# Decode attention over 16 heads: one column of one V block loaded by sixteen row transfers

## The chip, the cores and the metric

The kernel runs on one core of a Trainium2 chip. The metric is the device time of one execution in microseconds (us), the median of several runs. The core has a matrix engine (TensorE, PE in the profile; PEld is its loading of weights), a vector engine (VectorE, DVE), a scalar engine (ScalarE, ACT), GpSimd (POOL) and SyncE (SP). Each takes its own instruction stream in order, and they wait for each other through semaphores. Transfers between HBM (the device memory) and SBUF (the on-chip memory of 128 partitions) are issued by an engine's queue and carried out by 16 DMA engines.

## The reference

One query per head attends over 8192 keys, for 16 heads of width 256, in bf16:

```python
B, H, Sq, Sk, D = 1, 16, 1, 8192, 256
scale = q.shape[-1] ** -0.5
scores = jnp.einsum("bhqd,bhkd->bhqk", q, k) * scale
p = _softmax(scores, axis=-1)
return jnp.einsum("bhqk,bhkd->bhqd", p, v)
```

K and V are 4 MB per head each, 134 MB in all, and every byte is used once.

## The kernel before

**Layout.** For one head, the 8192 rows of K or of V are laid over the 128 partitions, 64 rows to a partition (`J = 64`). A partition so holds 64 "columns" of 256 bf16 values, 512 bytes each, which lie side by side in HBM too: a whole head is 32 KB per partition. There are two buffers for K and two for V (`kbuf`, `vbuf`), and head `h` uses buffer `h % 2`.

**Loads.** SyncE issues all loads of K and V in the order of the list `stream` (lines 57 to 69), in the loop at lines 128 to 138. For heads 2 to 15 it first issues the K of the head two further on, then the V of the head itself. Before the first part of a V it waits until the weighted sum of the head that used the buffer before is done (line 135, semaphore `pv`); so V of head 13 waits for the sum of head 11, V of head 14 for head 12, V of head 15 for head 13. Most V blocks come in one transfer. Head 13 (`V_HALVED`, line 16) comes in two halves of 32 columns, with the semaphores `va1` and `v1h`; head 14 in four pieces of 16 columns; head 15 in seven pieces that begin at columns 0, 16, 32, 44, 52, 58 and 62 (`V_LATE`, line 17). Every transfer covers all 128 partitions and raises its semaphore by 16 when it has landed. Behind the last part of V of head 13, the next thing in SyncE's list is the first piece of head 14, with its wait.

**Scores.** VectorE multiplies 48 of the 64 columns of K by the query and sums each (`head`, line 189). TensorE transposes the other 16 columns, four at a time (`ktrans`), ScalarE copies them out of PSUM (`evac`), and TensorE multiplies them by the query (`kscore`).

**Softmax and weighted sum.** The maximum, the exponentials `E` and their sum are made between the engines in small steps. Then `pv` (line 250) runs 64 matmuls on TensorE, one for each column of V, which add up in PSUM. Ahead of column `j` TensorE waits for what `waits` lists for `j`. ScalarE scales the result and stores it with a transfer of one row of 512 bytes (line 399).

**Order on TensorE.** The loop at line 339 runs nine turns. A turn has the scores of an even head, the weighted sum of the even head two before, the scores of an odd head, and the weighted sum of the odd head two before. The last turn has only the sums of heads 14 and 15. The waits are the same instructions in every turn; which count they wait for is worked out from the turn (`fin_turn`, `half_turn`), and GpSimd raises the semaphores at the start (lines 164 to 167), so that a wait which has no transfer in a turn is met at once. In the sum of an odd head the waits stand ahead of columns 16, 32, 44, 52, 58 and 62 for head 15's pieces, and ahead of column 32 for the second half of head 13.

Of the kernel before, what the change touches and what calls it, by code (L numbers as in the profile page):

```python
# [11 lines left out]
NPE = 16  # L12
# [28 lines left out]
def bass_standalone__mha_softmax__decode_kernel(nc: bass.Bass, q: bass.AP, k: bass.AP, v: bass.AP, out: bass.AP):  # L41
    B, H, Sq, D = q.shape
    Sk = k.shape[2]
    P = 128
    J = Sk // P
# [6 lines left out]
    HALF = J // 2  # L52
# [4 lines left out]
    stream = [("k", 0, 0, K_FIRST, "k0"), ("k", 0, K_FIRST, J, "k0b"), ("k", 1, 0, J, "k1")]  # L57
    stream += [("v", 0, 0, HALF, "va0"), ("k", 2, 0, J, "k0"), ("v", 0, HALF, J, "v0c")]
    stream += [("v", 1, 0, HALF, "va1"), ("k", 3, 0, J, "k1"), ("v", 1, HALF, J, "v1c")]
    for h in range(2, H):  # L60
        if h + 2 < H:
            stream.append(("k", h + 2, 0, J, f"k{h % 2}"))
        if h in V_LATE:
            for (a, b), name in zip(zip(V_LATE[h], V_LATE[h][1:] + (J,)), V_SEMS[h % 2]):
                stream.append(("v", h, a, b, name))
        elif h == V_HALVED:
            stream += [("v", h, 0, HALF, "va1"), ("v", h, HALF, J, "v1h")]
        else:
            stream.append(("v", h, 0, J, f"va{h % 2}"))

    with contextlib.ExitStack() as ctx:
# [9 lines left out]
        def sem(name):  # L81
            if name not in sems:
                sems[name] = ctx.enter_context(nc.semaphore(name))
            return sems[name]
# [29 lines left out]
        for name in ("l", "rc", "pv", "fin", "ldq", "k0", "k0b", "k1", "va0", "va1", "v1h", "o0", "o1"):  # L114
            sem(name)
        late = [name for row in V_SEMS for name in row[1:] if name not in ("v0c", "v1c")] + ["v1h"]
        for row in V_SEMS:
            for name in row[1:]:
                sem(name)

        def src(t, h):
            return t[0, h].rearrange("(p j) d -> p (j d)", p=P)

        if True:

            @(lambda f: f(nc.sync))
            def _(sp):
                for kind, h, a, b, name in stream:
                    buf = (kbuf if kind == "k" else vbuf)[h % 2]
                    if h >= 2 and a == 0:  # L130
                        if kind == "k":
                            sp.wait_ge(sem("kd"), h)
                            sp.wait_ge(sem("tp"), (h - 1) * NG)
                        else:
                            sp.wait_ge(sem("pv"), h + 1)
                    sp.dma_start(  # L136
                        buf[:, a * D : b * D], src(k if kind == "k" else v, h)[:, a * D : b * D]
                    ).then_inc(sem(name), 16)
                sp.nop()

            @(lambda f: f(nc.gpsimd))
            def _(pool):
                def step(ins, n):
                    ins.then_inc(sem("pool"), 1)
                    pool.wait_ge(sem("pool"), n)

                def eye(t, n, done):
                    step(pool.memset(t[:, :], 0.0), n)
                    pool.affine_select(
                        out=t[:, :],  # L150
                        in_=t[:, :],
                        compare_op=ALU.not_equal,
                        fill=1.0,
                        base=0,
                        pattern=[[-1, P]],
                        channel_multiplier=1,
                    ).then_inc(sem(done), 1)

                eye(identb, 1, "cb")
                eye(ident, 2, "cf")  # L160
                pool.memset(ones_row[:, :], 1.0).then_inc(sem("cf"), 1)
                pool.memset(ones_col[:, :], 1.0).then_inc(sem("cf"), 1)
                pool.memset(q_all[:, H * QW : (H + 1) * QW], 0.0).then_inc(sem("cf"), 1)
                for name, n in AHEAD.items():
                    pool.nop().then_inc(sem(name), n)
                for name in late + ["o0", "o1", "va0", "va1"]:
                    pool.nop().then_inc(sem(name), 32 if name in ("o0", "o1") else 16)

# [54 lines left out]
            def _(pe):  # L223
                def transpose_m(h):
                    pe.wait_ge(sem("m"), h.of(1, 2))
                    pe.matmul(  # L226
                        mx[0:1, 0:P], lhsT=m[:, h.par : h.par + 1], rhs=ident[:, :], start=True, stop=True
                    ).then_inc(sem("mT"), 1)

                def bcast(h):  # L230
                    pe.wait_ge(sem("g"), h.of(1, 2))
                    pe.matmul(  # L232
                        sm[:, 0:1],
                        lhsT=ones_row[0:1, 0:P],
                        rhs=g[0:1, h.par : h.par + 1],
                        start=True,
                        stop=True,
                    ).then_inc(sem("bc"), 1)

                def total(h):  # L240
                    pe.wait_ge(sem("ex"), h.of(1, 3))
                    pe.matmul(  # L242
                        qps[0:1, 0:1],
                        lhsT=lsum[:, h.par : h.par + 1],
                        rhs=ones_col[:, 0:1],
                        start=True,
                        stop=True,
                    ).then_inc(sem("l"), 1)

                def pv(h, waits, at):  # L250

                    pe.wait_ge(sem("fin"), h.of(1, 3))
                    pe.wait_ge(sem(f"va{h.par}"), h.of(8, 32 - 8 * h.par))
                    for j in range(J):
                        for name, value in waits.get(j, ()):
                            pe.wait_ge(sem(name), value)
                        ins = pe.matmul(  # L257
                            acc[h.par][0:1, 0:D],
                            lhsT=E[h.par][:, j : j + 1],
                            rhs=vbuf[h.par][:, j * D : (j + 1) * D],  # L260
                            start=(j == 0),
                            stop=(j == J - 1),
                        )
                        if j == J - 1:
                            ins.then_inc(sem("pv"), 1)
                        if j + 1 in at:
                            at[j + 1]()
# [33 lines left out]
                def scores(t, before=None):  # L301
                    if before:
                        transpose_m(before)
                    for gi in range(NG):
                        ktrans(t, gi)
                        if gi >= 1:
                            kscore(t, gi - 1)
                        if gi == 1 and before:
                            bcast(before)
                    kscore(t, NG - 1)  # L310
                    if before:
                        total(before)
# [26 lines left out]
                with pe.Fori(0, H // 2 + 1) as i:  # L339
                    ev, od = _Step(0, i), _Step(1, i)  # L340
                    fin_turn = pe.snap((i // 8) * 16 + 16)
                    half_turn = pe.snap(((i + 1) // 8) * 16 + 16)
                    old = od.back(2)
                    with pe.If(i < H // 2):
                        scores(ev)
                    with pe.If(i > 0):
                        pv(
                            ev.back(2),
                            {V_LATE[14][n]: [(V_SEMS[0][n], fin_turn)] for n in range(1, len(V_SEMS[0]))},
                            {32: lambda: transpose_m(old), 48: lambda: bcast(old), 64: lambda: total(old)},  # L350
                        )
                    with pe.If(i < H // 2):
                        scores(od, before=ev)
                    with pe.If(i > 0):
                        waits = {V_LATE[15][n]: [(V_SEMS[1][n], fin_turn)] for n in range(1, len(V_SEMS[1]))}
                        waits[HALF].append(("v1h", half_turn))
                        pv(old, waits, {})

            @(lambda f: f(nc.scalar))
# [120 lines left out]
```

## Time and profile before

| | us |
|---|---|
| median of 3 runs | 320.71 (320.42 to 320.89) |
| the profiled execution | 321.04 |
| its span, from the first to the last instruction | 319.6 |
| TensorE busy in the span | 220.9 (69%) |
| VectorE busy | 274.9 (86%) |
| ScalarE busy | 92.0 (29%) |

How to read the rows. Line numbers are those of the kernel (L257 is line 257). "out<-in" names what an instruction writes and reads. SPq and ACTq are the queues in which SyncE and ScalarE issue transfers. In the chain of waits and in a timeline the first number is the start in us from the span's start, the second the length, and x32 says that 32 instructions are merged. In a list of issues the last number is the time from the issue to the landing. In a row of stretches stand the stretch, its length, the busy time and the count of PE, PEld, DVE, ACT and POOL, then the granted TensorE clock as a share of full speed, the busy share of the DMA engines, and GB/s. In a row for one source line, three numbers with slashes are the shortest, the median and the longest duration in ns.

### The profile page before, as it was taken

How to read it: one execution, taken by the hardware profiler on the slowest of the kernel's cores; microseconds unless marked ns; L12 is line 12 of the kernel's file. 1: busy time of each engine (PE TensorE's matmuls, PEld its weight loads, DVE VectorE, ACT ScalarE, POOL GpSimd, SP SyncE). 2: the span in 40 equal slices, each digit the busy share in tenths (PEclk: the TensorE clock that was granted, in tenths of full speed). 3: DMA queues.
4: the chain of work that ended last, by engine and by line, in shares of the span. 5: the costliest groups of instructions: out<-in, count | busy, mean ns of one | idle time of the engine just before them, and what ended most of it. 6: DMA issues, size and time to landing. Idle time of an engine off the chain costs nothing.

```text
span 319.6 us, 6845 instructions
## 1 busy us (share of the span) xinstructions
PE 220.9 (69%) x2162; PEld 156.3 (49%) x2162; DVE 274.9 (86%) x1584; ACT 92.0 (29%) x171; POOL 1.6 (0%) x11
## 2 busy tenths in 40 slices
PE   4427186797875947849297573966749477397997
PEld 1326154565554635626256352653626355265675
DVE  2799999999999998897979979889797997979910
ACT  5436050433224060510506123060231605116010
POOL 1000000000000000000000000000000000000000
PEclk9999999769598786969769598785969969587799
DMA  8999999999999999999999999999999999999994
GB/s 329 451 397 455 392 453 416 416 427 435 439 418 443 431 435 439 418 439 427 439 435 423 439 418 443 431 431 435 427 439 414 447 435 427 439 406 423 422 399 179
DMA packets 6549, 134.29 MB, mean 420 GB/s; under 512 B 752, under 2 KB 912, under 8 KB 1424
## 3 DMA queue, kind: packets, MB, share of 16 engines
q1 hardware_dynamic: 6480, 134.22, 98.3%
q8 instruction: 2, 0.03, 0.0%
q10 hardware_dynamic: 64, 0.02, 0.0%
q14 instruction: 3, 0.02, 0.0%
HBM read 134.23 MB, written 0.01 MB: 420 GB/s over the span
## 4 chain that ended last, share of the span: by engine, by line
DMA 49%; PE 24%; DVE 23%; issue 2%; ACT 1%; ACTq 0%; SPq 0%; DVEq 0%
DMA vbuf<-in_v_dram 45%; PE acc L257 23%; DVE kbuf L189 22%; DMA kbuf<-in_k_dram 4%; DVE S L189 1%; PE sm L232 1%; ACT KT L367 1%; PE mx L226 0%; ACT o_sb L392 0%; ACT q_now L362 0%; DVE g L173 0%; SPq L136 0%; PE spe L292 0%; ACTq L399 0%; DVE recip L178 0%
## 5 line engine op out<-in xcount | busy, mean ns | idle before, releaser
L189 DVE CUSTOM_DVE_ANT_0 kbuf<-kbuf,q_now 128x256 bf16<-128x256 bf16 x768 | 268.1, 413 | 22.2 <-DMA kbuf<-in_k_dram 21.2
L257 PE MATMUL acc<-vbuf,E 128*1 128x256 bf16 x1024 | 147.6, 315 | 36.3 <-DMA vbuf<-in_v_dram 36.3
L257 PEld LDWEIGHTS acc<-vbuf,E 128*1 128x1 bf16 x1024 | 96.7, 96 | 80.4 <-DMA vbuf<-in_v_dram 37.3
L367 ACT ACTIVATE KT<-tp 128x1024 bf16<-128x1024 bf16 x64 | 63.8, 1018 | 30.3 <-PE tp L278 30.1
L189 DVE DVE_READ_ACCUMULATOR2_ANT S<- 128x1 f32 x768 | 58.4, 76 | 0.0
L278 PE MATMUL tp<-identb,kbuf 128*128 128x128 bf16 x512 | 42.3, 239 | 13.9 <-DMA kbuf<-in_k_dram 13.8
L292 PE MATMUL spe<-q_now,KT 128*128 128x1 bf16 x512 | 23.1, 166 | 32.3 <-ACT KT L367 31.6
L278 PEld LDWEIGHTS tp<-identb,kbuf 128*128 128x128 bf16 x512 | 33.5, 107 | 18.3 <-DMA kbuf<-in_k_dram 12.4
L292 PEld LDWEIGHTS spe<-q_now,KT 128*128 128x128 bf16 x512 | 18.0, 100 | 42.0 <-ACT KT L367 32.0
L392 ACT ACTIVATE o_sb<-acc,recip 1x256 bf16<-1x256 f32 x16 | 7.4, 464 | 99.9 <-PE acc L257 98.6
L375 ACT ACTIVATE negb<-sm 128x1 f32<-128x1 f32 x16 | 2.8, 172 | 84.5 <-PE sm L232 84.5
L173 DVE TENSOR_REDUCE g<-mx 1x1 f32<-1x128 f32 x16 | 4.4, 276 | 9.8 <-PE mx L226 9.8
L226 PE MATMUL mx<-ident,m 128*1 128x128 f32 x32 | 6.3, 279 | 5.7 <-DVE m L206 5.7
L232 PE MATMUL sm<-g,ones_row 1*128 1x1 f32 x32 | 6.2, 262 | 4.1 <-DVE g L173 4.1
L232 PEld LDWEIGHTS sm<-g,ones_row 1*128 1x128 f32 x32 | 4.9, 190 | 6.2 <-DVE g L173 4.7
L362 ACT ACTIVATE q_now<-q_all 128x258 bf16 (+1 forms) x17 | 7.0, 412 | 0.3 <-DVE S L189 0.3
L178 DVE RECIPROCAL recip<-qps 1x1 f32<-1x1 f32 x16 | 2.4, 151 | 3.9 <-PE qps L242 3.9
L379 ACT ACTIVATE E<-S,negb 128x64 bf16<-128x64 f32 x16 | 5.6, 348 | 0.5
L226 PEld LDWEIGHTS mx<-ident,m 128*1 128x1 f32 x32 | 2.2, 83 | 6.3 <-DVE m L206 5.9
L329 PE MATMUL acc<-q_sb,identb 16*128 16x256 bf16 x16 | 4.4, 403 | 1.0 <-ACT q_all L412 1.0
L371 ACT ACTIVATE S<-spe 128x16 f32<-128x16 f32 x16 | 2.9, 183 | 7.3 <-PE spe L292 7.3
L412 ACT ACTIVATE q_all<-acc 128x512 bf16<-128x512 f32 x8 | 4.4, 593 | 0.9 <-PE acc L329 0.9
(20 smaller groups left out, 16.6 us busy)
## 6 DMA issues: line engine op xcount, KB each, us to landing
kbuf<-in_k_dram SPq DMA_DIRECT2D x15, 4096.0 KB, 20.5
vbuf<-in_v_dram SPq DMA_DIRECT2D x11, 4096.0 KB, 29.0
vbuf<-in_v_dram SPq DMA_DIRECT2D x6, 2048.0 KB, 24.4
vbuf<-in_v_dram SPq DMA_DIRECT2D x6, 1024.0 KB, 12.8
kbuf<-in_k_dram SPq DMA_DIRECT2D x1, 3072.0 KB, 11.7
kbuf<-in_k_dram SPq DMA_DIRECT2D x1, 1024.0 KB, 4.8
vbuf<-in_v_dram SPq DMA_DIRECT2D x1, 768.0 KB, 9.1
vbuf<-in_v_dram SPq DMA_DIRECT2D x1, 512.0 KB, 9.9
```

What stands on the lines that cost most here:

```text
L173: dve.tensor_reduce(g[0:1, h.par : h.par + 1], mx[0:1, 0:P], AX.X, ALU.max).then_inc(sem("g"), 1)
L189: ins = dve.tensor_tensor_reduce(out=buf[:, j * D : (j + 1) * D], in0=buf[:, j * D : (j + 1) * D], in1=q_now[h.par][:, 0:D], scale=SCALE, ...
L226: pe.matmul(mx[0:1, 0:P], lhsT=m[:, h.par : h.par + 1], rhs=ident[:, :], start=True, stop=True).then_inc(sem("mT"), 1)
L232: pe.matmul(sm[:, 0:1], lhsT=ones_row[0:1, 0:P], rhs=g[0:1, h.par : h.par + 1], start=True, stop=True,).then_inc(sem("bc"), 1)
L257: ins = pe.matmul(acc[h.par][0:1, 0:D], lhsT=E[h.par][:, j : j + 1], rhs=vbuf[h.par][:, j * D : (j + 1) * D], start=(j == 0), stop=(j == J ...
L278: ins = pe.transpose(tp[gi % 2][:, b * D + hf * P : b * D + (hf + 1) * P], buf[:, j * D + hf * P : j * D + (hf + 1) * P], identb[:, :],)
L292: ins = pe.matmul(spe[:, c : c + 1], lhsT=KT[gi % 2][:, b * D + hf * P : b * D + (hf + 1) * P], rhs=q_now[h.par][:, D + hf : D + hf + 1], ...
L329: ins = pe.matmul(acc[pair % 2][:, (h % 2) * D : (h % 2 + 1) * D], lhsT=identb[0:H, h : h + 1].to_broadcast([H, P]), rhs=q_sb[:, :], start ...
L362: act.activation(out=q_now[h.par][:, :], in_=src_q, func=ACT.Copy).then_inc(sem("qb"), 1)
L367: act.activation(out=KT[gi % 2][:, :], in_=tp[gi % 2][:, :], func=ACT.Copy).then_inc(sem("kt"), 1)
L379: act.activation(out=E[h.par][:, :], in_=S[h.par][:, :], func=ACT.Exp, bias=negb[:, h.par : h.par + 1], scale=1.0, accum_out=lsum[:, h.par ...
L392: act.activation(out=o_sb[h.par][0:1, :], in_=acc[h.par][0:1, 0:D], func=ACT.Copy, scale=recip[0:1, h.par : h.par + 1],).then_inc(sem("fin ...
```

## The change

The second half of V of head 13 loses its last column, and that column (128 partitions by 512 bytes) comes behind it in sixteen transfers over 1, 2, 3 and so on to 15 partitions and at last over 8, which are 128 together. They share a new semaphore, `dg`, which they raise by 256 in all. TensorE waits for it ahead of the 64th column in the sum of every odd head; GpSimd raises it by 256 at the start for the turns before.

```diff
         elif h == V_HALVED:
-            stream += [("v", h, 0, HALF, "va1"), ("v", h, HALF, J, "v1h")]
+            stream += [("v", h, 0, HALF, "va1"), ("v", h, HALF, J - 1, "v1h")]
+            stream.append(("rows", h, J - 1, J, "dg"))
...
+        sem("dg")
...
+                    if kind == "rows":
+                        r = 0
+                        for n in list(range(1, NPE)) + [8]:
+                            sp.dma_start(
+                                buf[r : r + n, a * D : b * D], src(v, h)[r : r + n, a * D : b * D]
+                            ).then_inc(sem(name), 16)
+                            r += n
+                        continue
...
+                pool.nop().then_inc(sem("dg"), 256)
...
+                    rows_turn = pe.snap(((i + 1) // 8) * 256 + 256)
...
                         waits[HALF].append(("v1h", half_turn))
+                        waits[J - 1] = [("dg", rows_turn)]
```

## The prediction

> **What bounds the kernel now.** I read the page first, then the chain of waits over the last 80 us, then the issues of SyncE's queue one by one with their time to landing, and last the matmuls of the final heads.
>
> ```profile
> span 319.6 us, 6845 instructions
> ...
> DMA  8999999999999999999999999999999999999994
> ...
> DMA packets 6549, 134.29 MB, mean 420 GB/s; under 512 B 752, under 2 KB 912, under 8 KB 1424
> ...
> q1 hardware_dynamic: 6480, 134.22, 98.3%
> ...
> q10 hardware_dynamic: 64, 0.02, 0.0%
> ```
>
> Over the whole span the 16 DMA engines are the bound: SyncE's queue (q1) keeps them 98.3% busy. At 420 GB/s one engine moves 420/16 = 26 GB/s, so 512 B take it 0.02 us. But the change touches only head 13 and what comes behind it, so the question is what bounds the last 45 us:
>
> ```profile
> 247.26 29.66 DMA vbuf<-in_v_dram
> ...
> 276.97 6.03 PE acc L257 x32
> ...
> 293.47 13.27 PE acc L257 x96
> ...
> 310.88 7.02 PE acc L257 x64
> ...
> 317.98 0.47 ACT o_sb L392
> ```
>
> The last transfer on this chain is the V of head 12 (issued at 247.26, landed 29.66 us later). From 276.97 on, the chain is TensorE's work and some copies of ScalarE: the weighted sums of heads 12, 13, 14 and 15 one after another, with the scores of head 15 between. No transfer behind head 12's V stands in it. How near do those transfers come? First the matmuls of heads 13 and 15, and the stretch across the end of head 13:
>
> ```profile
> 293.43 9.82 PE L257 MATMUL acc<-vbuf,E 128*1 128x256 bf16 x64
> ...
> 302.87 3.87 PE L257 MATMUL acc<-vbuf,E 128*1 128x256 bf16 x34
> ...
> 310.74 7.15 PE L257 MATMUL acc<-vbuf,E 128*1 128x256 bf16 x64
> ...
> 293.40:303.00 9.60, 9.60 (x66) 6.38 (x65) 9.60 (x57) 0.17 (x1) 0.00 (x0) 0.71 1.00 416
> ...
> 298.95:303.20 4.25, 4.25 (x41) 3.27 (x40) 4.25 (x25) 0.00 (x0) 0.00 (x0) 1.00 1.00 414
> ```
>
> One matmul lasts 0.27 us and they overlap, so head 15's 64 columns start every (7.15 - 0.27)/63 = 0.109 us: column c at 310.74 + 0.109c. Head 13 is slower, 9.82 us, since the granted clock (the third number from the right) was 0.71 over its stretch and 1.00 only from 298.95 on; its last column starts at 293.43 + 9.82 - 0.27 = 302.98. Now the transfers, issue by issue (start and length of the issue, then size and us to landing):
>
> ```profile
> 266.95 0.43 SPq L136 DMA_DIRECT2D vbuf<-in_v_dram  x1
> vbuf<-in_v_dram SPq DMA_DIRECT2D x1, 2048.0 KB, 29.5
> ...
> 287.14 0.33 SPq L136 DMA_DIRECT2D vbuf<-in_v_dram  x1
> vbuf<-in_v_dram SPq DMA_DIRECT2D x1, 1024.0 KB, 11.8
> ...
> 288.46 0.43 SPq L136 DMA_DIRECT2D vbuf<-in_v_dram  x1
> vbuf<-in_v_dram SPq DMA_DIRECT2D x1, 1024.0 KB, 17.9
> ...
> 303.28 0.33 SPq L136 DMA_DIRECT2D vbuf<-in_v_dram  x1
> ...
> 305.28 0.44 SPq L136 DMA_DIRECT2D vbuf<-in_v_dram  x1
> vbuf<-in_v_dram SPq DMA_DIRECT2D x1, 384.0 KB, 10.2
> ...
> 305.76 0.45 SPq L136 DMA_DIRECT2D vbuf<-in_v_dram  x1
> vbuf<-in_v_dram SPq DMA_DIRECT2D x1, 256.0 KB, 10.3
> ...
> 306.25 0.45 SPq L136 DMA_DIRECT2D vbuf<-in_v_dram  x1
> vbuf<-in_v_dram SPq DMA_DIRECT2D x1, 128.0 KB, 10.1
> ```
>
> The second half of head 13's V lands at 266.95 + 29.5 = 296.45; its 64th column is used at 302.98, **6.5 us later**. Head 14's first piece lands at 298.9 and can't be used before 303.09, 4.2 us later; its last lands at 288.46 + 17.9 = 306.4 and is used at 303.09 + 48 x 0.109 = 308.3 at the earliest, 1.9 us later. In head 15 the 384 KB piece (columns 52 to 57) lands at 315.5 for a start at 316.4, the 256 KB piece at 316.1 for 317.1, the 128 KB piece at 316.35 for 317.5. So the smallest cover in the tail is about **0.95 us**, and a delay of all transfers behind head 13 shows in the end only beyond it.
>
> **The change part by part.**
>
> The half transfer of head 13 loses one column in 32: 128 rows of 512 B, 8 rows an engine, 8 x 0.02 = **-0.16 us** on every engine. Nobody waits for this half at its landing.
>
> Sixteen transfers come onto q1 right behind it: 128 data packets of 512 B, and a completion packet for each engine that takes part. How many take part is seen at two ends only: the 752 packets under 512 B are 45 transfers of SyncE by 16 (720), 16 for the load of q, and one for each of the 16 stores of one row, so 128 rows report from 16 engines and one row from one. Evenly spread, an engine gets 8 rows; in the worst case one engine gets all 128. I take sixteen rows for the busiest, one of each transfer, which is what follows if every transfer begins at the same engine and gives one row to each. [...]
>
> The price of one row with its completion: bytes alone, 0.02 us, are the lower end. The upper end is the 128 KB piece: it lands 316.35 - 316.06 = 0.29 us, say 0.3, behind the 256 KB one, and within that each engine wrote 8 packets of 1 KB and one completion. A pair of one packet and one completion can't be shown from it to cost less than 0.3, though 0.3/8 = 0.04 us is what a packet cost with its share. I take **0.04**: 128 KB at 420 GB/s are 0.31 us, so the completion left no time over. Busiest engine: 16 x 0.04 - 0.16 = **+0.48 us**, between 16 x 0.02 - 0.16 = +0.16 and 16 x 0.3 - 0.16 = +4.6; with 128 rows on one engine at 0.04 it is 5.1 - 0.16 = +5.0. The work that hides +0.48 is TensorE's queue of matmuls in heads 13, 14 and 15, by the 6.5, 1.9 and 0.95 us above; without that cover it is 0.48 us on the end. On the path: **0**.
>
> ```profile
> L136 SPq DMA_DIRECT2D vbuf<-in_v_dram x28: 327/432/643, 2.1 to 306.3; - x28
> ...
> L399 ACTq DMA_DIRECT2D out_dram<-o_sb x16: 230/231/493, 61.0 to 318.5; - x16
> ...
> L256 PEldq FUSED_REGOPS  x24: 83/83/97, 45.5 to 313.2; - x24
> ...
> L167 POOLq EVENT_SEMAPHORE  x12: 17/17/17, 2.8 to 3.7; - x12
> ```
>
> SyncE issues sixteen more transfers. A one-row transfer takes ScalarE's queue 0.23 us, SyncE's own take 0.33 to 0.64: 3.7 to 10.2 us, and 16 x 0.43 = 6.9 by the median. The last one before them ends at 266.95 + 0.43 = 267.38 and the next thing on SyncE is head 14's first piece, which goes at 287.14, when head 12's sum is done. 19.8 us of waiting stand there, so each issue may cost 1.23 us before head 14 is late at all. Path: **0**.
>
> TensorE waits once more in every odd head, ahead of its 64th column, at 0.083 us of its sequencer each. Queued behind it are that head's last matmul, the signal that lets SyncE load head 15, and the next head. In all odd heads but 13 the count was reached before, so only the instruction is left. Two fall into the tail, heads 13 and 15: 0.17 us if nothing covered them. But the stretch from 302.87 crosses the end of head 13, the loop's turn and head 14's first wait and still has (3.87 - 0.27)/33 = 0.109 us a matmul, like head 15 with its six waits: the sequencer runs ahead. Path: 0, at most 0.17; I take **0.05**. GpSimd's extra signal is 0.017 us at 3 us; the first such wait comes at 45.5.
>
> Sum: 0 + 0 + 0.05. On the profiled execution (321.04 us, of which 319.6 are the span) 321.1; this run lies 0.33 over the median of 320.71, so the forecast is **320.8 us, no change that shows**.
>
> [...]
>
> **The rivals.**
>
> *Completions that don't overlap (slower).* On one engine a new completion may follow only when the one before has been taken. For: nothing in the trace puts completions closer than 0.3 us apart on an engine within q1. Against: there eight packets stood between and time was left for none. It decides from (0.95 + 0.16)/16 = 0.07 us a pair, if the busiest engine is also the last; at 0.3 the end moves by 4.6 - 0.95 = 3.7 us, to 324.4.
>
> *A queue that takes only so many transfers (slower).* At 306.25 eight are under way (head 14's last and seven of head 15), and no issue is longer than 0.64. The change has up to 20: head 12's V, head 15's K, two halves and sixteen. With room for eight, only four small ones go in at once, the others as landings make room, the last behind 296.45; then head 14's pieces are issued near 300 instead of from 287.14, the engines stand empty about 5 us, and the end comes 5 - 0.95 = 4 us later, 324.7. Against: nothing shows such a bound.
>
> *Sixteen transfers one behind the other (slower, far).* A transfer alone takes this long:
>
> ```profile
> q_sb<-in_q_dram ACTq DMA_DIRECT2D x1, 8.0 KB, 2.9
> ```
>
> In a row they would end at 296.45 + 16 x 2.9 = 342.9; the 64th column is wanted at 302.98, so 360. The pieces of head 15, landing 0.3 to 0.6 apart after 10 us each, speak against it.
>
> *Faster.* The engines that get fewer than 8 of the 128 rows are done up to 0.16 us sooner. That is under 0.1% even if the end hung on them, and it does not: 0.95 us of TensorE lie over it. A real gain needs the clock: from 293.43 to 298.95 head 13 ran at half speed, where 5.5 us gave the work of 2.8, so a shifted low stretch could give up to 2.7 us, 318.0. Against: the change leaves TensorE's idle times as they are, and the three runs lie within 0.47 us. That the added edits do nothing seen is the forecast itself.
>
> **How the numbers follow.** Forecast 0.73, completions 0.14, bounded queue 0.06, one behind the other 0.02, clock 0.05. About 0.2% (0.64 us) is what a measurement tells from no change. Of the forecast 0.70 stay within it, 0.02 above, 0.01 below; of the clock case 0.04 below, 0.01 within. Slower 0.02 + 0.14 + 0.06 + 0.02 = 0.24, same 0.71, faster 0.05. The forecast's own range is 320.2 to 321.3; to hold 8 in 10 it is stretched over the lower half of the first rival, to 323.0.
>
> **What would show it.** In the new profile: small packets up from 752 by 128 if every row reports from its own engine (q1 6480 + 256); sixteen short issues behind 267.4, done before 279; head 13's last small transfer landing before 302.98; head 14's first issue still at the end of head 12's sum; the chain from 276.97 on TensorE's alone. Wrong if the 64th column waits for a transfer, if head 15's pieces land over 0.95 us later, or if the tail gets or loses a stretch of low clock.

## The result, and the profile after

The changed kernel takes 321.9 us (median of 19 runs, 321.72 to 322.26) against 320.47 us for the kernel before (19 runs on the same chip). The ratio is 1.0038, 95% interval 1.0029 to 1.0047: slower by 0.9 to 1.5 us, which is small but beyond the 0.2% that can be told from no change. The profiled execution agrees: its span is 320.5 us, 0.9 us longer. The lowest of the 19 times is 1.60 us above the lowest before (320.12), the highest only 0.28 us above the highest before (321.98).

The page of the changed kernel counts the packets:

```profile
span 320.5 us, 6870 instructions
...
DMA packets 6805, 134.29 MB, mean 419 GB/s; under 512 B 880, under 2 KB 1168, under 8 KB 1680
...
q1 hardware_dynamic: 6736, 134.22, 98.2%
```

880 packets under 512 B are 752 + 128, and 6736 on SyncE's queue are 6480 + 256: each of the 128 rows brings one data packet and one completion packet. The bytes are the same.

SyncE's timeline from 264 us on, and the chain of waits over the last 72 us, of the changed kernel:

```profile
267.27 5.63 SPq L141 DMA_DIRECT2D vbuf<-in_v_dram  x16
286.99 19.50 SPq L146 DMA_DIRECT2D vbuf<-in_v_dram  x11
```

```profile
248.76 28.18 DMA vbuf<-in_v_dram
...
276.99 5.86 PE acc L268 x32
...
293.32 9.70 PE acc L268 x64
...
303.04 0.33 SPq L146
...
303.41 9.70 DMA vbuf<-in_v_dram
...
313.15 1.91 PE acc L268 x16
315.06 0.13 issue
315.19 3.67 PE acc L268 x32
318.93 0.46 ACT o_sb L405
```

SyncE needs 5.63 us for the sixteen issues (0.35 each) and is done at 272.9; head 14's first piece goes at 286.99, as before (287.14). Up to 293.32 the chain is that of before. Then a transfer stands in it that was not there: one issued at 303.41, the second piece of head 15, which lands at 313.11. In the kernel before, that piece had this row (its issue, and behind it its size and time to landing):

```profile
303.65 0.43 SPq L136 DMA_DIRECT2D vbuf<-in_v_dram  x1
vbuf<-in_v_dram SPq DMA_DIRECT2D x1, 1024.0 KB, 7.7
```

It landed at 311.35. TensorE's timeline of the changed kernel shows what the later landing does:

```profile
310.67 1.91 PE L268 MATMUL acc<-vbuf,E 128*1 128x256 bf16 x16
313.15 5.69 PE L268 MATMUL acc<-vbuf,E 128*1 128x256 bf16 x48 [0.57 <-DMA vbuf<-in_v_dram]
```

Head 15 starts at 310.67 (before 310.74). Column 16 would start at 310.67 + 16 x 0.109 = 312.41 and starts at 313.15, 0.74 us late; the last 48 columns then take 5.69 us where 47 x 0.109 + 0.27 = 5.39 would do, because the later pieces are late too. Head 15's matmuls end at 318.84, and before at 317.89. That is the whole 0.95 us.

Which transfers are late? Issues of the changed kernel one by one, as the prediction showed them for before:

```profile
266.80 0.43 SPq L146 DMA_DIRECT2D vbuf<-in_v_dram  x1
vbuf<-in_v_dram SPq DMA_DIRECT2D x1, 1984.0 KB, 29.7
...
288.33 0.43 SPq L146 DMA_DIRECT2D vbuf<-in_v_dram  x1
vbuf<-in_v_dram SPq DMA_DIRECT2D x1, 1024.0 KB, 19.8
...
306.04 0.44 SPq L146 DMA_DIRECT2D vbuf<-in_v_dram  x1
vbuf<-in_v_dram SPq DMA_DIRECT2D x1, 128.0 KB, 12.1
```

The second half of head 13 lands at 296.5 as before (296.45). Head 14's last piece lands at 308.13 (before 306.36) and head 15's last at 318.14 (before 316.35): **everything behind the sixteen lands about 1.8 us later**, and the amount neither grows nor shrinks from head 14 to head 15. So it is lost at one place. Three stretches, the first of the changed kernel alone, the others of both, changed kernel first:

```profile
290.00:293.50 3.50, 2.33 (x44) 1.75 (x43) 3.50 (x21) 2.92 (x7) 0.00 (x0) 0.75 1.00 427
293.50:296.50 3.00, 3.00 (x16) 1.78 (x15) 3.00 (x19) 0.00 (x0) 0.00 (x0) 0.50 1.03 331
296.50:300.00 3.50, 3.50 (x24) 2.31 (x23) 3.50 (x21) 0.00 (x0) 0.00 (x0) 0.70 0.97 382
```

```profile
293.50:296.50 3.00, 3.00 (x15) 1.78 (x15) 3.00 (x19) 0.07 (x1) 0.00 (x0) 0.50 0.94 396
296.50:300.00 3.50, 3.50 (x23) 2.23 (x21) 3.50 (x21) 0.00 (x0) 0.00 (x0) 0.65 1.01 421
```

The last two numbers are the busy share of the DMA engines and the GB/s. Where the small transfers pass, the engines count as fully busy but move 331 and 382 GB/s instead of 396 and 421. Over these 6.5 us that is (65 x 3.0 + 39 x 3.5) = 332 KB less, 0.8 us at 420 GB/s as a mean over 16 engines; the last engine is 1.8 us late. A busy share of 1.03 at 331 GB/s, against 0.94 at 396 before, says here that an engine holds a packet, not that bytes flow. The trace's records of single packets show which are held. In the changed kernel a packet of 512 B takes 0.027 us and a completion 0.009 (before: 0.009), and such pairs pass as little as 0.03 us apart; but an 8 KB packet of head 14 behind them takes up to 1.63 us, where none took more than 0.32 over the same stretch (293 to 304 us) in the kernel before. Behind 304 us single packets take up to 0.9 us in both kernels.

### The profile page after: what moved, and what is told of

It is laid out like the page before. It is cut to its first block, busy times and chain, and to the rows that moved or that the text cites. A ratio compares the mean times of both kernels' runs of the same rounds, so it can differ in the third digit from the quotient of the medians.

```text
span 320.5 us, 6870 instructions
## 1 busy us (share of the span) xinstructions
PE 220.1 (69%) x2162; PEld 155.5 (49%) x2162; DVE 274.9 (86%) x1584; ACT 91.9 (29%) x171; POOL 1.6 (0%) x11
## 3 DMA queue, kind: packets, MB, share of 16 engines
q1 hardware_dynamic: 6736, 134.22, 98.2%
## 4 chain that ended last, share of the span: by engine, by line
DMA 51%; DVE 23%; PE 22%; issue 2%; ACT 1%; SPq 0%; ACTq 0%; DVEq 0%
DMA vbuf<-in_v_dram 48%; DVE kbuf L200 22%; PE acc L268 20%; DMA kbuf<-in_k_dram 4%; DVE S L200 1%; PE sm L243 1%; ACT KT L380 1%; PE mx L237 0%; SPq L146 0%; ACT o_sb L405 0%; ACT q_now L375 0%; DVE g L184 0%; PE spe L303 0%; ACTq L412 0%; DVE recip L189 0%
## 5 line engine op out<-in xcount | busy, mean ns | idle before, releaser
L289 PE MATMUL tp<-identb,kbuf 128*128 128x128 bf16 x512 | 41.5, 237 | 14.5 <-DMA kbuf<-in_k_dram 14.5
```

Source lines behind the costliest of these rows:

```text
L289: ins = pe.transpose(tp[gi % 2][:, b * D + hf * P : b * D + (hf + 1) * P], buf[:, j * D + hf * P : j * D + (hf + 1) * P], identb[:, :],)
```

## The experiments

What is compared is **the lag**: the landing of head 14's last piece less the landing of head 12's V, both in the same profiled execution, so that a shift ahead of head 12 drops out. It is 306.36 - 276.92 = 29.44 us before and 308.13 - 276.94 = 31.19 after. The lag of an experiment, less 29.44, is what its edit costs the transfers. Times and lags of all runs follow, with the ratio to the kernel before on the same chip. That kernel's own median lay between 320.47 and 321.32 on the chips used, so medians of different rows are not compared:

| run | what column 64 of head 13 does | lag | median | ratio (95%) |
|---|---|---|---|---|
| before | part of the half | 29.44 | 320.47 | |
| changed | 16 transfers, 1 to 15 and 8 rows | 31.19 | 321.90 | 1.0038 (1.0029 to 1.0047) |
| e1_waits | part of the half; only TensorE's wait added | 29.42 | 320.89 | 0.9999 (0.9979 to 1.0020) |
| e2_one | 1 transfer, 128 rows | 29.53 | 320.71 | 0.9997 (0.9979 to 1.0015) |
| e3_even8 | 8 transfers, 16 rows each | 30.31 | 321.50 | 1.0016 (0.9999 to 1.0033) |
| e4_row1 | 16 transfers of 1 row, 1 of 112 | 30.18 | 321.09 | 1.0006 (0.9992 to 1.0021) |
| e5_sems | as e3_even8, a semaphore each | 30.24 | 321.15 | 1.0004 (0.9988 to 1.0020) |
| e6_wide | last 16 columns in 8 transfers of 16 rows | 33.39 | 325.32 | 1.0136 (1.0107 to 1.0165) |
| e7_double | columns 63 and 64, 32 transfers | 33.06 | 324.28 | 1.0109 (1.0083 to 1.0134) |
| e8_early | the 16 transfers in head 5 | 29.44 | 322.19 | 1.0038 (1.0020 to 1.0056) |
| e9_stride | as e5_sems, every eighth row | 30.09 | 321.17 | 1.0019 (1.0009 to 1.0029) |
| e10_wide_stride | as e6_wide, every eighth row | 33.56 | 324.11 | 1.0112 (1.0090 to 1.0134) |
| e11_spread | the 16 transfers in four groups | 30.00 | 321.61 | 1.0037 (1.0018 to 1.0057) |
| e12_eight | last 16 columns in 8 transfers of 8 rows, half of the partitions left out | 29.14 | 320.66 | 0.9981 (0.9961 to 1.0001) |

The theory after the result: the price of a completion on its engine was set too low. Its rivals: TensorE's added wait and register work; the small packets themselves; the number of completions in all; the semaphore that all share, or neighbouring rows; and, where sizes differ, the bytes.

**e1_waits.** The loads go back to two halves, and GpSimd meets the wait of all turns; TensorE's instructions stay.

```diff
-            stream += [("v", h, 0, HALF, "va1"), ("v", h, HALF, J - 1, "v1h")]
-            stream.append(("rows", h, J - 1, J, "dg"))
+            stream += [("v", h, 0, HALF, "va1"), ("v", h, HALF, J, "v1h")]
...
-                pool.nop().then_inc(sem("dg"), 256)
+                pool.nop().then_inc(sem("dg"), 512)
```

> Only TensorE's extra wait ahead of each 64th column and its register work stay; the column comes with the second half again, as before, and no small transfer is issued. Completion theory (each completion that an engine must write for a tiny transfer costs it about 0.19 us): nothing is left that costs, ratio 1.000 within 0.001, and the last piece of V of head 14 lands 29.4 us behind the V of head 12, as before (changed kernel: 31.2). Rival, the wait and register work on TensorE: the whole loss stays, ratio 1.003 to 1.004.

The lag is 29.42 and the ratio 0.9999. The wait costs nothing that shows; the interval leaves room for 0.6 us.

**e2_one.** Column 64 keeps its own 128 packets of 512 B, but in one transfer.

```diff
+ROWS = (128,)
...
-                        for n in list(range(1, NPE)) + [8]:
+                        for n in ROWS:
```

> The 64th column comes in one transfer over 128 rows: 8 packets of 512 B and one completion on each engine, 128 small packets in all as in the change. Completion theory: 8 x 0.02 - 0.16 and one completion, +0.0 to +0.2 us: the last piece of head 14 lands 29.4 to 29.7 us behind the V of head 12, ratio 1.000 to 1.001. Rival, small packets cost (0.19 us each, 8 on every engine): +1.4 us, 30.8, ratio 1.002 to 1.004.

The list of issues of this run, and the row of head 14's last piece:

```profile
vbuf<-in_v_dram SPq DMA_DIRECT2D x1, 64.0 KB, 28.4
...
287.43 0.43 SPq L147 DMA_DIRECT2D vbuf<-in_v_dram  x1
vbuf<-in_v_dram SPq DMA_DIRECT2D x1, 1024.0 KB, 18.9
```

The 64 KB land, and the lag is 29.53, +0.09 us. So 128 small packets as such, eight on an engine, are nearly free.

This execution shows one thing more. The second piece of head 15 stands in its chain of waits (first row), and TensorE waits for it (second row, from its timeline), though it lands no later than in the kernel before (311.34 and 311.35):

```profile
301.61 9.73 DMA vbuf<-in_v_dram
...
311.38 5.68 PE L269 MATMUL acc<-vbuf,E 128*1 128x256 bf16 x48 [0.57 <-DMA vbuf<-in_v_dram]
```

It took 320.21 us, the execution from which the prediction read its 0.95 us of cover 321.04. Here the granted clock over 293.40 to 303.00 was 0.82 instead of 0.71 and head 15's sum began at 308.91 instead of 310.74, so column 16 could have started at 308.91 + 16 x 0.109 = 310.65, ahead of its transfer. **In this execution the tail has no cover at all.**

**e3_even8.** The same 128 packets in eight transfers of 16 rows: still eight data packets on an engine, but eight completions in place of one.

```diff
+ROWS = (16,) * 8
```

> The 64th column comes in eight transfers over 16 rows: one packet and one completion on every engine each time, 8 of both per engine, no engine busier than another. Completion theory: 8 x 0.19 - 0.16 = +1.4 us on every engine, the last one too: head 14's last piece 30.8 us behind the V of head 12, ratio 1.001 to 1.003. If some completions are free and only those beyond the first eight or so cost: +0.1 to +0.3 us, 29.5 to 29.8, ratio 1.000. Rival, unequal loading of the engines as the cause: nothing, 29.4.

The lag is 30.31, +0.87 us: between the two that were expected, 30.8 and 29.5 to 29.8. That the first eight would be free is not borne out. Against e2_one only seven more completions (with their transfers) have come onto each engine: (0.87 - 0.09)/7 = **0.11 us each**.

**e4_row1.** Sixteen transfers of one row, and the other 112 rows in one: one engine gets 17 completions, the others far fewer in all.

```diff
+ROWS = (1,) * 16 + (112,)
```

> Sixteen transfers of one row each and one over 112 rows: 32 completions in all in place of 128, but 17 of them on one engine. Completion theory: the one engine is as late as in the change, 17 x 0.19 - 0.16 = 3.1 us, so head 14's last piece lands about 31.3 us behind the V of head 12 (changed kernel 31.2), ratio 1.003 to 1.005. Rival, the count of all completions: a quarter of the loss, 29.9, ratio 1.001. Rival, small packets (23 on that engine): 23 x 0.19 = 4.4 us, some 32.6, ratio 1.007 or more.

The lag is 30.18, +0.74 us: below what the busiest engine alone should cost, and above 29.9, which the number of all completions would give. The lag decides for neither, but the semaphore events of the trace say more. Among the 32 landings on `dg` is one row of 17, from 294.89 to 297.88, in steps of 0.18 to 0.21 us, **0.187 in the mean**, as one engine with 17 completions gives them (no record numbers the engines); the other 15 lie between 294.45 and 296.73. So, by this reading, the pace holds on one engine alone. That engine was also early: its share of the second half had landed by 294.71, the last engine's at 296.53. Of the 3.1 us that were expected of it a lead of 1.8 leaves 1.3, and 0.74 show in the lag. One row was not expected, head 14's fourth piece:

```profile
287.81 2.53 SPq L147 DMA_DIRECT2D vbuf<-in_v_dram  x1
vbuf<-in_v_dram SPq DMA_DIRECT2D x1, 1024.0 KB, 19.3
```

Its issue took 2.53 us instead of 0.43: see the last section.

**e5_sems and e9_stride.** The eight transfers of e3_even8 with a semaphore each, so that every landing can be seen; then the same with rows r, r + 8, r + 16 and so on instead of 16 neighbours.

```diff
+        DG = [f"dg{n}" for n in range(8)]
+        for name in DG:
+            sem(name)
...
-                        for n in list(range(1, NPE)) + [8]:
+                        for n, name in zip(ROWS, DG):
...
+                for name in DG:
+                    pool.nop().then_inc(sem(name), 16)
...
-                        waits[J - 1] = [("dg", rows_turn)]
+                        waits[J - 1] = [(name, half_turn) for name in DG]
```

```diff
-                                buf[r : r + n, a * D : b * D], src(v, h)[r : r + n, a * D : b * D]
+                                buf[r : P : 8, a * D : b * D], src(v, h)[r : P : 8, a * D : b * D]
```

> The eight transfers over 16 rows of the run before, but each with a semaphore of its own, so that each landing is seen by itself. Completion theory (an engine lets its completions out one by one, whatever semaphore they raise): the eight land 0.18 to 0.20 us apart, the last about 1.4 us behind the first, and head 14's last piece 30.3 us behind the V of head 12, as with the shared semaphore. Rival, one semaphore raised from many sides is the narrow place: the landings lie 0.03 to 0.05 us apart, the pace of the packets themselves, and head 14's last piece comes at 29.4 to 29.6.

> As the run with eight semaphores, but each of the eight transfers over 16 rows takes every eighth row instead of 16 neighbours, so that the 16 engines write all over the partitions. Completion theory: which rows they are doesn't matter, the landings stay 0.18 to 0.20 us apart and head 14's last piece comes 30.2 us behind the V of head 12. Rival, 16 engines that write into 16 neighbouring partitions get in each other's way: the landings come closer, under 0.12 us apart, and head 14's last piece at 29.7 or below.

The first and the last of the eight in e5_sems, issue and landing:

```profile
268.39 0.43 SPq L144 DMA_DIRECT2D vbuf<-in_v_dram  x1
vbuf<-in_v_dram SPq DMA_DIRECT2D x1, 8.0 KB, 28.3
...
271.64 0.42 SPq L144 DMA_DIRECT2D vbuf<-in_v_dram  x1
vbuf<-in_v_dram SPq DMA_DIRECT2D x1, 8.0 KB, 26.3
```

They are issued up to 3.25 us apart and land at 296.7 and 297.9, seven steps of **0.18 us**. The bytes of such a transfer, one packet of 512 B on an engine, would take 0.02 us at 420/16 = 26 GB/s. With every eighth row the landings lie 0.17 us apart:

```profile
268.16 0.54 SPq L144 DMA_DIRECT2D vbuf<-in_v_dram  x1
vbuf<-in_v_dram SPq DMA_DIRECT2D x1, 8.0 KB, 28.6
...
272.53 0.59 SPq L144 DMA_DIRECT2D vbuf<-in_v_dram  x1
vbuf<-in_v_dram SPq DMA_DIRECT2D x1, 8.0 KB, 25.4
```

The lags, 30.24 and 30.09, are those of e3_even8 within 0.25 us. So neither the shared semaphore nor the neighbouring rows set the pace. The times don't bear out that 0.7 to 0.9 us of lag vanish in the 0.95 us of cover: e5_sems is not told from the kernel before (1.0004), but e9_stride is slower (1.0019, interval 1.0009 to 1.0029), and in the profiled executions of both TensorE waits for head 15's second piece, as in e2_one. The row of e9_stride:

```profile
312.08 5.77 PE L272 MATMUL acc<-vbuf,E 128*1 128x256 bf16 x48 [0.57 <-DMA vbuf<-in_v_dram]
```

**e7_double.** Columns 63 and 64 both in sixteen transfers.

```diff
-            stream += [("v", h, 0, HALF, "va1"), ("v", h, HALF, J - 1, "v1h")]
-            stream.append(("rows", h, J - 1, J, "dg"))
+            stream += [("v", h, 0, HALF, "va1"), ("v", h, HALF, J - 2, "v1h")]
+            stream += [("rows", h, J - 2, J - 1, "dg"), ("rows", h, J - 1, J, "dg")]
```

> Columns 63 and 64 both come in the sixteen transfers of the change, 30 to 32 completions on the two busiest engines in place of 15 and 16. Completion theory: 15 or 16 more at 0.19 us, less 0.16 for the bytes taken from the half: +2.7 us on top of the change, head 14's last piece near 33.9 us behind the V of head 12 (change 31.2), all of it on the end: ratio 1.011 to 1.014. Rival, one stall of fixed size per burst: 31.2, ratio 1.004. Rival, a bound on transfers under way (36 here, 20 in the change): SyncE's issues stretch and head 14 is issued late.

The lag is 33.06, +3.62 us: twice the 1.75 of sixteen. Adding back the bytes that leave the half (0.16 us a column, by the prediction), the price of a pair on the busiest engine is (0.87 + 0.16)/8 = 0.13 in e3_even8, (1.75 + 0.16)/16 = 0.12 in the changed kernel and (3.62 + 0.32)/32 = 0.12 here. SyncE's timeline shows a second thing:

```profile
268.27 21.03 SPq L142 DMA_DIRECT2D vbuf<-in_v_dram  x32
289.34 15.37 SPq L147 DMA_DIRECT2D vbuf<-in_v_dram  x11
```

32 issues take 21.03 us, 0.66 each instead of 0.35, and head 14's first piece goes 2.2 us later than in the kernel before. The lag is what the price above gives without this, so it is not shown to have cost anything.

**e8_early.** The sixteen transfers go behind V of head 5, eight heads ahead of the end; head 13 has its two halves again.

```diff
-            stream += [("v", h, 0, HALF, "va1"), ("v", h, HALF, J - 1, "v1h")]
-            stream.append(("rows", h, J - 1, J, "dg"))
+            stream += [("v", h, 0, HALF, "va1"), ("v", h, HALF, J, "v1h")]
+        elif h == V_ROWS:
+            stream += [("v", h, 0, J - 1, "va1"), ("rows", h, J - 1, J, "dg")]
...
-                    rows_turn = pe.snap(((i + 1) // 8) * 256 + 256)
+                    rows_turn = pe.snap(((i + 5) // 8) * 256 + 256)
```

> The sixteen transfers stand behind V of head 5 in place of head 13; head 13 comes in halves as before. There the end of the DMA stream sets the pace, with no cover of TensorE's. Completion theory: the late engine stays late through all later transfers, the V of head 12 lands up to 1.8 us later than before (276.9), between 277.3 and 278.7 by how far the busiest engine was ahead of the last, and the end moves by the same: ratio 1.001 to 1.0055. Rival, the engines make up for it in the eight heads that follow: nothing, ratio 1.000.

The chain of this run:

```profile
249.27 29.57 DMA vbuf<-in_v_dram
...
278.89 6.14 PE acc L270 x32
...
312.97 7.02 PE acc L270 x64
```

V of head 12 lands at 278.84 instead of 276.92, 1.9 us late, and head 15 starts its sum 2.1 us late; the lag within the tail is 29.44, as before. Not all of the 1.9 us is the small transfers': V of head 5, which comes ahead of them, already landed 0.3 us late in this execution (141.2 instead of 140.9). The next full block behind them, K of head 8, has this row:

```profile
130.96 0.36 SPq L148 DMA_DIRECT2D kbuf<-in_k_dram  x1
kbuf<-in_k_dram SPq DMA_DIRECT2D x1, 4096.0 KB, 21.5
```

It lands at 152.4 instead of 150.6, 1.8 us late. So the sixteen cost **about 1.5 us** at their place, and seven heads later that is still there (1.9 less 0.3). It is not made good in these seven heads; SyncE's queue kept the engines busy for 98.3% of the span before and 98.2% in the changed kernel, which left next to no idle time in which it could be. Here V of head 12 stands in the chain itself, so there is no cover. The ratio is 1.0038, some 1.2 us, between 0.6 and 1.8 by its interval; this profiled execution took 323.28 us, above the median of its runs.

**e11_spread.** The sixteen in groups of 5, 5, 3 and 3, behind the two halves of head 13 and the first two pieces of head 14.

```diff
+                if (h, a) in ((14, 0), (14, 16)):
+                    stream.append(("rows", 13, 10 + 3 * (a // 16), 13 + 3 * (a // 16), "dg"))
...
-            stream += [("v", h, 0, HALF, "va1"), ("v", h, HALF, J - 1, "v1h")]
-            stream.append(("rows", h, J - 1, J, "dg"))
+            stream += [("v", h, 0, HALF, "va1"), ("rows", h, 0, 5, "dg")]
+            stream += [("v", h, HALF, J - 1, "v1h"), ("rows", h, 5, 10, "dg")]
```

> The sixteen transfers of the change, the same rows and the same 128 completions, but not in one burst: five behind each half of head 13, three behind each of the first two pieces of head 14. Completion theory (a burst costs 0.19 us for each completion on the busiest engine, less about 0.8 us that the engine reads ahead meanwhile): at most five in a row, 0.0 to 0.4 us a burst and mostly hidden, head 14's last piece 29.4 to 30.2 us behind the V of head 12, ratio 1.000 to 1.002. Rival, each small transfer costs a fixed time wherever it stands: 31.2 as in the change, ratio 1.004.

The lag falls to 30.00, +0.56 us for the same sixteen transfers: (0.56 + 0.16)/16 = 0.045 us a pair, against 0.12 in one burst. This is as expected, though the 0.8 us that the expectation takes off a burst was the author's estimate, and no run shows an engine reading ahead. The ratio, 1.0037, is not as expected. The chain shows why:

```profile
289.99 12.92 DMA vbuf<-in_v_dram
...
302.95 0.28 PE acc L271
...
303.99 3.65 PE acc L271 x32
...
311.78 7.02 PE acc L271 x64
```

The last small transfer, now issued behind head 14's second piece, lands at 302.91, when TensorE is about to use column 64. In the kernel before, TensorE's sequencer had run ahead past the loop's turn: its branches there (L339 to L346) stand at 301.1 to 302.0, ahead of column 64 at 302.98, and the matmuls from 302.87 on follow at 0.109 us. Here it did not, behind a wait that was met only at 302.91. Column 64 starts at 302.95 and head 14's sum at 303.99, 1.04 us behind it, where it was 0.11 before (302.98 and 303.09). The chain names ScalarE's copy of head 13's result between the two, but by the kernel's counts head 14 needs only the copy of head 12; from 302.95 to 303.94 the trace has the branches and register work of the loop's turn on TensorE's sequencer. The delay moved from the transfers to the end of head 13.

**e6_wide, e10_wide_stride and e12_eight.** The completions again, but with 8 KB on an engine ahead of each: the last sixteen columns in eight transfers, over 16 neighbouring rows, over every eighth row, and, in e12_eight, over every fourth of 32 rows, eight rows each.

```diff
-            stream += [("v", h, 0, HALF, "va1"), ("v", h, HALF, J - 1, "v1h")]
-            stream.append(("rows", h, J - 1, J, "dg"))
+            stream += [("v", h, 0, HALF, "va1"), ("v", h, HALF, J - 16, "v1h")]
+            stream.append(("rows", h, J - 16, J, "dg"))
...
-                        waits[J - 1] = [("dg", rows_turn)]
+                        waits[J - 16] = [("dg", rows_turn)]
```

e10_wide_stride takes its rows as e9_stride does, and e12_eight so, with a semaphore each:

```diff
+ROWS = (0, 1, 2, 3, 32, 33, 34, 35)
...
+                                buf[r : r + 32 : 4, a * D : b * D], src(v, h)[r : r + 32 : 4, a * D : b * D]
```

> Again eight transfers over 16 rows, but over the last 16 columns instead of one: each engine moves 8 KB, 0.31 us, between two completions. As many completions as in the two runs before. Completion theory (they must be closer than about 0.19 us to cost anything): no loss, head 14's last piece 29.4 to 29.6 us behind the V of head 12, ratio 0.999 to 1.001. Rival, each completion costs the engine a fixed time wherever it stands: +0.9 us as there, 30.3, ratio 1.0015.

> As the run with 16 columns in eight transfers over 16 rows, which lost 4 us, but with every eighth row. If its loss came from many engines writing into few neighbouring partitions, the loss falls to some +1 to +2 us: head 14's last piece 30.5 to 31.5 us behind the V of head 12 (there 33.4, before 29.4). If the loss came from the eight completions, or from 16-row transfers as such, it stays at 33.4. [...]

> The last 16 columns of head 13 come in eight transfers over 8 rows (every fourth of a block of 32), for the partitions 0 to 63 alone; for the partitions 64 to 127 these columns are left out, so 0.5 MB less is loaded. Each transfer has a semaphore of its own and 8 KB a row, one row and one completion on each of eight engines, as in the two runs over 16 rows that lost 4 us, where a row with its completion took about 0.6 us. Theory A, a completion behind every 8 KB packet costs the engine what it cost there: the eight landings lie 0.5 to 0.6 us apart. [...]

The stretch in which these transfers pass, one row of each run in this order:

```profile
293.00:299.00 6.00, 5.76 (x36) 3.57 (x37) 6.00 (x37) 0.37 (x2) 0.00 (x0) 0.50 1.02 221
```

```profile
293.00:299.00 6.00, 6.00 (x38) 3.69 (x39) 6.00 (x37) 0.18 (x1) 0.00 (x0) 0.52 1.02 212
```

```profile
293.00:299.00 6.00, 5.47 (x34) 3.36 (x35) 6.00 (x35) 0.66 (x2) 0.00 (x0) 0.50 1.01 421
```

e6_wide was expected to cost nothing, since 8 KB take 0.31 us and would cover a completion. It cost 3.95 us of lag, and the engines moved 221 GB/s: that expectation fell. So did the next, that neighbouring rows were the reason: with every eighth row it is 212 GB/s and +4.1 us. (The +1 to +2 us expected under it were the author's estimate.) In e12_eight the engines move 421 GB/s, the eight land 0.31 us apart by the trace's semaphore events (294.28, 294.59 and so on to 296.46), not the 0.5 to 0.6 that a price for each completion would give, and the lag is 29.14, although a completion still follows every 8 KB packet. That half of the partitions is left out doesn't explain it: if each of the eight rows goes over an engine of its own, as the changed kernel's one completion for each row suggests (128 more for 128 rows), the eight engines that take part carry a row of 8 KB from each transfer, 64 KB each, as much as these columns gave every engine before, and 8 KB in 0.31 us is 26 GB/s, the pace of the bytes (420/16). So **a completion behind each 8 KB is free** there, at a distance of 0.31 us, and what halves the rate in the other two is something else: it came with transfers of sixteen rows (221 and 212 GB/s) and did not come with eight rows of half the partitions (421). e12_eight changed the engines, the rows and the bytes at once, so which of them it is stays open. For the column of 64 KB such a half rate would add 0.15 us by estimate (64 KB at 212 instead of 420 GB/s), so it cannot be the 0.87 us of e3_even8 or the 1.75 of the change.

## Why the prediction was right, and where not

The time came within the range, but the result is that of the first rival, completions that don't overlap, not of the forecast. The forecast's own range, 320.2 to 321.3, doesn't hold it; the stretch to 323.0, made for that rival, does. The prediction's own sign of being wrong, pieces of head 15 over 0.95 us late, was met: they are 1.8 us late.

**What held.** The sixteen issues are done long before head 14 needs SyncE (5.6 us against 6.9 predicted, none longer than the 1.23 us allowed). The 128 rows report as assumed, with 128 more small packets; the second half lands when it did, and no matmul of head 13 waits. TensorE's wait and GpSimd's signal cost nothing that shows (e1_waits, lag 29.42 against 29.44). The second rival, a queue with room for few, and the third, one transfer behind the other, did not come in the changed kernel.

**What failed** are two terms. The first is the price: "I take 0.04: 128 KB at 420 GB/s are 0.31 us, so the completion left no time over." The row that this was read from has eight packets of 1 KB ahead of each completion. It shows a completion hidden behind 0.29 us of data, as e12_eight does behind 0.31, and says nothing of completions with 512 B between them. Those follow one another on an engine at 0.17 to 0.19 us (e4_row1, e5_sems, e9_stride), and what the stream behind them loses is 0.12 to 0.13 us a pair, the same for 8, 16 and 32. With 0.12 the prediction's own sum gives 16 x 0.12 - 0.16 = 1.76 us for the busiest engine, where it had +0.48. The sixteen rows on the busiest engine in that sum were an assumption, and no run numbers the engines; e4_row1 shows in its place a row of 17 landings 0.187 us apart, as sixteen transfers of one row and one of 112 give it when all of them use one engine. The rival, at 0.3 us a pair, had the price too high: the 0.3 us of the upper bound was that of the data (128 KB at 420 GB/s).

The second is the cover: "the smallest cover in the tail is about 0.95 us". It is right for the execution that it was read from: in the two profiled executions, both above their medians, 1.8 us of lateness less 0.95 is 0.85, and the span grew by 0.9. The wait fell on head 15's second piece, though, which the prediction had not listed: its cover was 310.74 + 16 x 0.109 - 311.35 = 1.13 us. But the cover is not the kernel's: e2_one has none, with the transfers where they were. The times of the 19 executions fit this. From the lowest to the lowest the change costs 1.60 us, nearly the whole lag, and from the highest to the highest 0.28. That it was 0.95 us in the middle, and that 320.8 + 1.76 - 0.95 = 321.6 comes near the measured 321.9, is in part luck: the profiled execution was one with much cover.

The same 64 KB cost +0.09 us of lag in one transfer (e2_one) and +1.75 in sixteen (the change). The record of a completion packet has 0.009 us in the kernel before and in the changed one, yet the landings lie 0.17 to 0.19 us apart with eight or more in close order on one engine; whether the write of the semaphore or something else of a transfer takes that time, no run here shows.

**What stays open.** Every added completion came with a transfer of its own, so these runs don't part the completion from what else a transfer brings to an engine. Why a pace of 0.18 us costs the stream only 0.12, and why the early engine of e4_row1 costs 0.74 us and not 1.3, no row here shows. How much cover an execution has was seen in a few profiles and not set by any run.

## What to carry to other kernels

In e12_eight a completion cost nothing that shows where 8 KB, or 0.31 us, lay between it and the next on the same engine (lag 29.14 against 29.44; with as much between them in transfers of sixteen rows the rate halved to 212 to 221 GB/s, for a reason left open). Small transfers in close order landed 0.17 to 0.19 us apart and cost the stream 0.12 to 0.13 us a pair on the busiest engine (e3_even8, the change, e7_double). So count completions per engine and per burst, not bytes or packets. In e8_early, with the DMA engines busy for some 98% of the span, a delay of about 1.5 us was still there seven heads later; in the change 1.8 us of lateness showed in the profiled execution as 0.9, less the cover that the compute had over the last transfers. A cover read from one execution holds for that execution: look at a second one, whose clock fell otherwise (over 293.40 to 303.00 it was 0.71 with 0.95 us of cover before, 0.82 with none in e2_one). A price read from one row holds for the distances in that row alone: look what covered it there.

## What was not expected of the hardware

- Completions of small transfers in close order land about 0.18 us apart on one engine (0.187 in e4_row1), with a shared semaphore (e4_row1), one each (0.18 in e5_sems) or every eighth row (0.17 in e9_stride), while the engines count as busy: 331 GB/s at a busy share of 1.03 in the changed kernel. The packets themselves are recorded far closer, at 0.03 us, and the wait shows on the 8 KB packets behind them: up to 1.63 us, against 0.32 before.
- SyncE's issues did become slow in runs with more small transfers under way: 0.35 us each for sixteen (the change), 0.66 for 32 (e7_double), and 2.53 for one large piece behind the seventeen of e4_row1, where that piece took 0.43 before. What sets this was not tried.
- Transfers of sixteen rows by 8 KB ran the engines at 221 GB/s with sixteen neighbouring rows (e6_wide) and 212 with every eighth row (e10_wide_stride), half of the 421 of eight rows in half the partitions (e12_eight). No run here shows the reason.
- In e11_spread a wait that was met only at its last moment cost more than its lateness: the small transfer landed at 302.91, and head 14's sum started 1.04 us behind column 64 instead of 0.11, with the branches and register work of the loop's turn on TensorE's sequencer between, from 302.95 to 303.94, where before the branches had run by 302.0.
